# Attention whose products with v take float32 operands, in an order planned from a list of tasks

## The chip, the cores and the metric

The kernel runs on one core of a Trainium2 chip. The metric is the device time of one execution in microseconds (us). The engines are TensorE (PE, with its weight loads PEld), VectorE (DVE), ScalarE (ACT), GpSimd (POOL) and SyncE (SP), which issues the transfers (DMA). Each engine works through its own queue of instructions in the order in which the program was written.

## What is computed

Three blocks follow one another: attention over 4 batches of 12 heads (448 positions, 64 columns a head), a gated layer (768 to 1024, with a spatial product over the 448 positions), and a mixer (rank 32 over the positions, then 768 to 3072 and back).

```python
q_n, k_n = rmsnorm(q, g_q), rmsnorm(k, g_k)
scores = scale * (q_n @ k_n.T)
attn = exp(scores - max(scores))
x = (attn / (sum(attn) + 1e-9)) @ v        # 4 x 448 x 768
u, w = split(gelu(x @ w_in))               # 2 x 512
x = x + (u * (w_sg @ layernorm(w) * ... + b_sg)) @ w_out
t = x + (x.T @ U @ V).T
out = t + relu(t @ w_ch1) @ w_ch2
```

The large weights `w_in`, `w_out`, `w_ch1`, `w_ch2`, U and V arrive as float64 and are turned into float32 and then into two float16 halves on the chip (`from_f64`, `split_steps`). Nearly every large product is made of three products of float16 halves (high by high, high by low, low by high).

## The kernel before

**Units of attention.** A unit is a pair of heads of one batch: 24 units, 0 to 23. Its steps, in the names of the code: `load` and `load_v` (transfers for one to three units at a time), `sq` and `su` (squares on ACT, sums on DVE), `nw` (the reciprocal root, twelve steps on DVE, `rsqrt_steps`), `xn` (scaling, POOL), `ct` (eight float32 transposes of q and k on PE), `cq`, `ck`, `lq`, `lk` (their high halves on ACT, low halves on DVE), `cd` (eight transfers on SP that stack the halves into `kk` and `qq`), `mm` (eight matmuls that give an approximate maximum of each row of scores), `mr` (seven reductions on DVE), `mt`, `mn` (the maxima transposed, negated and sent into a row of `qq` by a transfer), `sc` (16 matmuls of the scores `st`), `se` (the exponential `e`, float32, on ACT), `sh` and `sl` (its halves `eh` on ACT and `el` on POOL), `va` and `vb` (the halves `vh` on ACT and `vl` on DVE of v, times 16, with a column of ones in `vh` for the sum), `pv` (96 matmuls into two banks, one a head: 8 groups of 128 output rows, each of 4 key blocks times 3 products) and `px` (the sum's reciprocal and the division into `XX`, DVE, for each head).

**Banks.** PE's results lie in 8 banks of 128 x 512 float32: the pool `ps` has 4 single banks (transposes, maxima and `pv` take turns), `pst` two tiles of two banks for the scores. When attention ends `pst` closes and a pool `ps2` of 2 banks takes its place.

**Order.** The table T of numbers gives each step of a unit a time, in units of `UT_` = 8.3 us; `at_unit` puts the step on a heap, and `issue()` takes the steps from the heap by time and writes their instructions. The first weights, the second half of `w_in` (`wv`: six tiles `wvh`, `wvl` of 128 x 512, which the first product behind attention needs), are spread over the times 21.12 to 23.715, that is, among the last units; their five conversion steps and both halves are on DVE (`alone`). The times of the work behind attention stand in the same table, and the stage of the mixer's last two products follows by rules of its own. Each tile converted by `from_f64` takes five operations: the absolute value or a mask, a clamp from below (L160), a shift, and two that join sign and low bits (L161 to L163).

Of the kernel before, what the change touches and what calls it, by code (L numbers as in the profile page):

```python
# [12 lines left out]
F16 = mybir.dt.float16  # L13
# [10 lines left out]
def attention_gmlp_mixer_kernel(  # L24
# [31 lines left out]
    P = 128  # L56
# [15 lines left out]
    ps = ctx.enter_context(tc.tile_pool(name="ps", bufs=4, space=PSUM))  # L72
# [9 lines left out]
    mhalf = const.tile([P, 14], F32, name="mhalf")  # L82
# [42 lines left out]

# [24 lines left out]
    def from_f64(m, z, alone):  # L150
        def f0():
            z["g"] = z["t"].bitcast(F32)
            if alone:
                nc.vector.tensor_scalar(out=z["t"], in0=z["d"][:, :, 1], scalar1=0x7FFFFFFF, scalar2=None, op0=ALU.bitwise_and)
            else:
                nc.scalar.activation(out=z["g"], in_=z["d"].bitcast(F32)[:, :, 1], func=AF.Abs)

        return [
            (dve2 if alone else act)(m, f0),
            dve2(m, lambda: nc.vector.tensor_scalar(out=z["g"], in0=z["g"], scalar1=2.0 ** -15 * 1.125, scalar2=None, op0=ALU.max)),  # L160
            dve2(m, lambda: nc.vector.tensor_scalar(out=z["t"], in0=z["t"], scalar1=3, scalar2=0x3FFFFFFF, op0=ALU.logical_shift_left, op1=ALU.bitwise_and)),  # L161
            dve(m, lambda: nc.vector.scalar_tensor_tensor(out=z["t"], in0=z["d"][:, :, 1], scalar=-0x40000000, in1=z["t"], op0=ALU.bitwise_and, op1=ALU.bitwise_or)),  # L162
            dve(m, lambda: nc.vector.scalar_tensor_tensor(out=z["w"].bitcast(I32), in0=z["d"][:, :, 0], scalar=29, in1=z["t"], op0=ALU.logical_shift_right, op1=ALU.bitwise_or)),  # L163
        ]
# [6 lines left out]

    def rsqrt_steps(y, x, t):

        yi, xi = y.bitcast(I32), x.bitcast(I32)
        steps = [
            lambda: nc.vector.tensor_scalar(out=yi, in0=xi, scalar1=1, scalar2=None, op0=ALU.logical_shift_right),
            lambda: nc.vector.tensor_scalar(out=yi, in0=yi, scalar1=-1, scalar2=0x5F3759DF, op0=ALU.mult, op1=ALU.add),
        ]
        return steps + 3 * [
            lambda: nc.vector.tensor_tensor(out=t, in0=y, in1=y, op=ALU.mult),  # L180
            lambda: nc.vector.scalar_tensor_tensor(out=t, in0=t, scalar=-0.5, in1=x, op0=ALU.mult, op1=ALU.mult),
            lambda: nc.vector.scalar_tensor_tensor(out=y, in0=t, scalar=1.5, in1=y, op0=ALU.add, op1=ALU.mult),
        ]
# [54 lines left out]

    def issue():


        rings = {x: SimpleNamespace(n=2, taken=[], back=set(), held=[]) for x in "dwx"}
# [4 lines left out]

        free = dict(V=0.0, A=0.0, G=0.0, D=0.0)
        done = set()
        running, waiting = [], []  # L250
        delay = 0.0
        heapq.heapify(jobs)
        while jobs or running:
# [14 lines left out]
            more.now = i  # L268
# [96 lines left out]
    def fp32_tile(name):  # L365
        return at.tile([P, 2 * S], F32, tag="e", name=name, bufs=EB)
# [943 lines left out]
```

## Time and profile before

| what | before |
|---|---|
| median of 2 runs | 1219.51 us (1218.91 to 1220.11) |
| the profiled execution | 1219.57 us, its span 1217.8 us |
| mean granted clock of PE | 0.972 |
| PE busy | 1152.3 us (95%) |
| PE weight loads busy | 627.4 us |
| DVE busy | 1017.6 us (84%) |
| ACT busy | 484.3 us (40%) |
| POOL busy | 390.6 us (32%) |

A row of a timeline has the start, the length, the engine, the line of the code, the operation, the tile written and the tiles read, the shape and the count; `x4` means that four neighbours stand in one row, whose length is that of all four. A group of rows by line has the busy time, the mean of one instruction, and the idle time of the engine ahead of it with what ended that. A window gives the busy time of each engine in a stretch, PE's granted clock (1.00 is full speed), the busy share of the 16 DMA engines and GB/s.

### The profile page before, as it was taken

Reading aid. Unit: us, or ns where it says so; the run is one execution under the profiler, and the core shown is the slowest. Engines: PE = TensorE matmul, PEld = TensorE weight load, DVE = VectorE, ACT = ScalarE, POOL = GpSimd, SP = SyncE. Lnnn points to the kernel's source line nnn. Section 1 sums busy time; section 2 is a strip of 40 time slices with the busy share of each in tenths; the row PEclk is TensorE's granted clock in tenths of the full one; section 3 lists DMA queues with packets and bytes.
Section 4 is the critical chain, followed back from the end, with each engine's and each line's share of the span. In section 5 each row is a group of like instructions: output and inputs, shape, how many; then the busy total and the mean of one; then the engine's idle time right before and its main releaser. Section 6 shows DMA issues by size and latency. Waiting matters only on the chain.

```text
span 1217.8 us, 20703 instructions
## 1 busy us (share of the span) xinstructions
PE 1152.3 (95%) x7914; PEld 627.4 (52%) x7914; DVE 1017.6 (84%) x2004; ACT 484.3 (40%) x850; POOL 390.6 (32%) x348
## 2 busy tenths in 40 slices
PE   8899999998579999996999999999999999999998
PEld 3355565554334454443445555555555555555554
DVE  6698999989988745789896998989879898898955
ACT  2677777765435322334342332323223232232200
POOL 3477777765333413674051111101111011110100
PEclk9799999998799999999999999999999999999999
DMA  5455544523546400435154222212222122212113
GB/s 139 118 131 132 124 110 117 130 72 106 137 113 139 119 1 1 95 84 115 25 117 91 63 87 73 69 49 74 61 62 58 59 67 69 61 57 61 44 65 117
DMA packets 134835, 103.88 MB, mean 85 GB/s; under 512 B 77328, under 2 KB 114896, under 8 KB 134736
## 3 DMA queue, kind: packets, MB, share of 16 engines
q1 hardware_dynamic: 134736, 102.56, 32.8%
q8 instruction: 62, 1.02, 0.4%
q14 instruction: 37, 0.30, 0.1%
HBM read 65.33 MB, written 5.51 MB: 58 GB/s over the span
## 4 chain that ended last, share of the span: by engine, by line
PE 67%; DVE 22%; DMA 4%; issue 3%; POOL 2%; ACT 2%; SPq 0%; DVEq 0%; ACTq 0%; POOLq 0%
PE pd L1172 8%; PE pd L1174 8%; PE pd L1173 8%; PE q L1111 7%; PE q L1112 6%; PE q L1113 6%; PE st L499 5%; PE pv L535 3%; PE pm L465 2%; DVE wt L162 2%; DVE ww L163 2%; DVE u L77 2%; PE won L361 2%; DVE wt L160 2%; DVE wt L161 1%
## 5 line engine op out<-in xcount | busy, mean ns | idle before, releaser
L1172 PE MATMUL pd<-w,hh 128*128 128x384 f16 x672 | 219.4, 326 | 2.6 <-ACT hh L1138 1.5
L1174 PE MATMUL pd<-w,hl 128*128 128x384 f16 x672 | 219.3, 326 | 1.3 <-DVE hl L1141 1.3
L1173 PE MATMUL pd<-w,hh 128*128 128x384 f16 x672 | 219.3, 326 | 0.5 <-DVE w L77 0.5
L1178 DVE SCALAR_TENSOR_TENSOR xx<-pd,xx 128x384 f32<-128x384 f32 x336 | 184.0, 551 | 25.9 <-PE pd L1174 23.0
L516 POOL TENSOR_TENSOR el<-e,eh 128x896 f16<-128x896 f32 (+1 forms) x96 | 165.3, 1733 | 69.5 <-ACT eh L510 62.0
L1111 PE MATMUL q<-u,w1h 128*128 128x448 f16 x504 | 178.7, 354 | 2.4 <-DMA u<-u 2.4
L1112 PE MATMUL q<-u,w1h 128*128 128x448 f16 x504 | 178.6, 354 | 0.0
L1113 PE MATMUL q<-u,w1l 128*128 128x448 f16 x504 | 178.5, 354 | 0.0
L1074 POOL TENSOR_TENSOR wt<-ww 128x256 f32<-128x256 f32 x36 | 27.3, 759 | 441.1 <-DVE ww L163 441.1
L536 PE MATMUL pv<-vl,eh 128*128 128x64 f16 (+1 forms) x768 | 113.3, 197 | 13.0 <-DVE vl L77 13.0
L1125 DVE TENSOR_TENSOR u<-q,u 128x448 f32<-128x448 f32 x144 | 87.7, 620 | 40.1 <-PE q L1113 38.0
L535 PE MATMUL pv<-vh,eh 128*128 128x65 f16 (+1 forms) x768 | 113.9, 201 | 0.0
L1138 ACT ACTIVATE hh<-u 128x448 f16<-128x448 f32 (+2 forms) x144 | 58.0, 445 | 136.9 <-DVE u L1125 136.8
L537 PE MATMUL pv<-vh,el 128*128 128x65 f16 (+1 forms) x768 | 112.1, 196 | 0.0
L470 DVE TENSOR_REDUCE mx<-pm 128x1 f32<-128x448 f32 x168 | 98.7, 619 | 12.3 <-PE pm L465 10.4
L499 PE MATMUL st<-qq,kk 128*128 128x448 f16 (+1 forms) x384 | 95.0, 384 | 0.3 <-DMA qq<-nm 0.3
L535 PEld LDWEIGHTS <-eh 128*128 128x128 f16 (+1 forms) x768 | 72.7, 98 | 40.6 <-issue 21.9
L1172 PEld LDWEIGHTS <-hh 128*128 128x128 f16 x672 | 65.6, 98 | 46.8 <-ACT hh L1138 2.3
L1174 PEld LDWEIGHTS <-hl 128*128 128x128 f16 x672 | 65.6, 98 | 46.5 <-DVE hl L1141 2.5
L1173 PEld LDWEIGHTS <-hh 128*128 128x128 f16 x672 | 65.6, 98 | 45.5 <-issue 2.2
L504 ACT ACTIVATE e<-st 128x896 f32<-128x896 f32 x96 | 77.1, 817 | 15.2 <-PE st L499 15.2
L510 ACT ACTIVATE eh<-e 128x896 f16<-128x896 f32 (+1 forms) x96 | 82.1, 855 | 0.2
(157 smaller groups left out, 2278.1 us busy)
## 6 DMA issues: line engine op xcount, KB each, us to landing
wd<-in_moe_w_ch_dram SPq DMA_DIRECT2D x36, 512.0 KB
wd<-in_moe_w_ch_dram SPq DMA_DIRECT2D x48, 384.0 KB
wd<-in_moe_w_in_dram SPq DMA_DIRECT2D x12, 512.0 KB
kk<-wk SPq DMA_DIRECT2D x48, 112.0 KB
qq<-wq SPq DMA_DIRECT2D x48, 112.0 KB
out_dram<-xx SPq DMA_DIRECT2D x12, 384.0 KB
raw<-in_q_dram SPq DMA_DIRECT2D x7, 576.0 KB
raw<-in_k_dram SPq DMA_DIRECT2D x7, 576.0 KB
```

Of the source, the lines that this page charges most:

```text
L499: nc.tensor.matmul(oo, kk[:, z, hh, cs], qq[:, z, hh, :], start=(z == 0), stop=(z == 1))
L516: (nc.vector if 4 * n + g in T["sd"] else nc.gpsimd).tensor_tensor(out=el[:, 0:m], in0=e, in1=Z[n][f"eh{g}"][:, 0:m], op=ALU.subtract)
L535: nc.tensor.matmul(o[:, g, :], ph, vh[kp, i, :], start=(kc == 0), stop=False)
L536: nc.tensor.matmul(o[:, g, 0:D], ph, vl[kp, i, :], start=False, stop=False)
L537: nc.tensor.matmul(o[:, g, :], pl, vh[kp, i, :], start=False, stop=(kc == 3))
L1111: nc.tensor.matmul(z[bank_], wh[:, c, b], uh[:, c], start=(c == 0), stop=False)
L1112: nc.tensor.matmul(z[bank_], wh[:, c, b], ul[:, c], start=False, stop=False)
L1113: nc.tensor.matmul(z[bank_], wl[:, c, b], uh[:, c], start=False, stop=(c == KH - 1))
L1172: nc.tensor.matmul(o[:, 0:HN], hh[:, m, ts], wh[:, m, ns], start=(m == GC - 1), stop=False)
L1173: nc.tensor.matmul(o[:, 0:HN], hh[:, m, ts], wl[:, m, ns], start=False, stop=False)
L1174: nc.tensor.matmul(o[:, 0:HN], hl[:, m, ts], wh[:, m, ns], start=False, stop=(m == 0))
L1178: then(e, [dve(HN, lambda z=z, ns=ns: nc.vector.scalar_tensor_tensor(out=X[i][:, ns], in0=z["o"][:, 0:HN], scalar=2.0 ** -14, in1=X[i][:, ...
```

## The change

- `pv` reads `e` and v as float32. A unit has 32 products in place of 96: 24 of 128 output rows and 8 of 64 rows, all of 65 columns, into one bank of 7 x 65 for both heads. `sh`, `sl`, `va` and `vb` are gone. Tiles `VR` hold v with its column of ones and with zeros where the half-height block of the other head stands; `load_v` needs five transfers in place of three.
- `px` runs once a unit for both heads.
- `ct` makes seven full transposes into one two-bank tile of `pst`. `mm` writes two blocks (i, i + 4) into a two-bank tile, `mr` reduces two banks at once (three of these, and one single).
- `nw` is two operations on POOL, the second a `pow`.
- `from_f64` loses the clamp: the first step multiplies by 2^-112 instead of taking the absolute value, so tiny values go to zero by themselves.
- `ps` has 2 banks, `pst` three tiles of two. Behind attention `ps2` and a new `ps3` take 2 banks each, and `bank` and `product` rotate over them.
- The order of attention comes from a list: `task(name, rank, engines, f, deps, ...)` names the step, its rank, the time it is taken to need on its engine, what must be done before, and which buffers of a counted ring it takes and gives back. `attention_order()` goes through time and starts, on each free engine, the ready task of the lowest rank. The six tiles of `wv` are chains of such tasks, with ranks spread over 21.12 to 23.715; their first step and high half are on ACT (`wva=0`). Ready tasks of lower rank go first, and where an engine would stand idle, a task of any rank may start. The times behind attention are moved by `SHIFT`, the planned end of attention less the old one; the next weights `wu` and `ws` wait until the last tile of `wv` is under way.

```diff
@@ from_f64
-                nc.scalar.activation(out=z["g"], in_=z["d"].bitcast(F32)[:, :, 1], func=AF.Abs)
+                nc.scalar.activation(out=z["g"], in_=src, func=AF.Copy, scale=2.0 ** -112)
-            dve2(m, lambda: nc.vector.tensor_scalar(out=z["g"], in0=z["g"], scalar1=2.0 ** -15 * 1.125, scalar2=None, op0=ALU.max)),
@@ load_v
-        dma(out=vr[:, :, 0:3, :], in_=v[b, h0:h0 + LH, 0:S3, :].rearrange("h (p c) d -> p h c d", c=3))
+        for c in range(3):
+            dma(out=vr[:, :, c, 0:D], in_=v[b, h0:h0 + LH, 0:S3, :].rearrange("h (p c) d -> p h c d", c=3)[:, :, c, :])
@@ nw
+        nc.gpsimd.tensor_scalar(out=ms, in0=ms, scalar1=1.0 / D, scalar2=1e-6, op0=ALU.mult, op1=ALU.add)
+        nc.gpsimd.tensor_tensor(out=y.rearrange("p u s -> p (u s)"), in0=ms, in1=mhalf[:, 0:14 * m], op=ALU.pow)
@@ ct
+        pt = pst.tile([P, 2, 512], F32, tag="st", name="pqk").rearrange("p a s -> p (a s)")
+        for o, c in ((0, 0), (1, 1), (2, 2), (3, 6), (4, 3), (5, 4), (6, 5)):
+            nc.tensor.transpose(out=pt[:, o * P:(o + 1) * P], in_=x[:, c, :], identity=ident)
@@ mm
+        pm = Z[n][f"pm{j}"] = pst.tile([P, 2, 512], F32, tag="st", name="pm")
+        for i in ((j, j + 4) if j < 3 else (3,)):
...
@@ pv
         for kc in range(4):
-            nc.tensor.matmul(o[:, g, :], ph, vh[kp, i, :], start=(kc == 0), stop=False)
-            nc.tensor.matmul(o[:, g, 0:D], ph, vl[kp, i, :], start=False, stop=False)
-            nc.tensor.matmul(o[:, g, :], pl, vh[kp, i, :], start=False, stop=(kc == 3))
+            for oo, e, cs in to:
+                i = 4 * e + kc if kc < 3 else 3
+                nc.tensor.matmul(oo, z[f"e{i // 2}"][:, i % 2, cs], v_[:, 4 * e + kc, :], start=(kc == 0), stop=(kc == 3))
@@ order
-    spread(UT_ * T["wv0"], UT_ * T["wv1"], wv[nw_:], T["wvl"], T["wvg"])
+        for g in range(4):
+            task(("sc", n, g), rk(f"s{g}", n), dict(P=(0.78, 0.97, 0.78, 0.4)[g]), lambda n=n, g=g: sc(n, g),
+                 [("md", n)] + [("cd", n, i) for i in range(4)], take=["st"])
...
+            task(("pv", n, hh, g), rk("ab"[hh] + str(g), n), dict(P=0.65 if g == 3 else 0.44), lambda n=n, hh=hh, g=g: pv(n, hh, g),
...
+    for c, steps in enumerate(wv):
+        chain(("wv", c), steps, T["wv0"] + (T["wv1"] - T["wv0"]) * c / KD, T["wvg"])
...
+    for t, x, e in (attn := attention_order())[0]:
+        at_time(t, x.f)
+    SHIFT = attn[1] - UT_ * T["te"]
```

PE's queue in the middle of attention, before: the products with v (`pv`) of one unit and a maximum's product (`pm`) of the next between two groups of them; a row is one instruction, and each matmul has its load of weights ahead of it.

```order
L537 LDWEIGHTS el
L537 MATMUL pv<-vh_110,el 128x65
L465 LDWEIGHTS wq
L465 MATMUL pm<-wk,wq 128x448
L535 LDWEIGHTS eh
L535 MATMUL pv<-vh_110,eh 128x65
L536 LDWEIGHTS eh
L536 MATMUL pv<-vl,eh 128x64
L537 LDWEIGHTS el
L537 MATMUL pv<-vh_110,el 128x65
```

PE's queue in the middle of attention, of the change: `vr_183` and `vr_184` are the v of two units, `pqk` the transposes of a later unit, `pmt` the transposed maxima.

```order
L523 MATMUL pv<-vr_183,e 128x65 x4
L503 LDWEIGHTS kk_98
L503 MATMUL st<-qq_101,kk_98 128x448
L503 LDWEIGHTS kk_98
L503 MATMUL st<-qq_101,kk_98 128x448
L523 MATMUL pv<-vr_183,e 64x65 x8
L424 MATMUL pqk<-ident,xn 128x128 x7
L476 MATMUL pmt<-ident,mx 7x128
L523 MATMUL pv<-vr_184,e 128x65 x4
L466 LDWEIGHTS wq
L466 MATMUL pm<-wk,wq 128x448
```

Twelve float16 products became four float32 ones (one row `x4`), the seven transposes stand in one row, and products of two units stand around each other.

DVE's queue among units 22 and 23, before: the five conversions and two halves of the first weights (L154 to L163, L114, L77) between the reductions `mx` of unit 23.

```order
L154 TENSOR_SCALAR wt<-wd 128x512
L470 TENSOR_REDUCE mx<-pm 128x1
L160 TENSOR_SCALAR wt<-wt 128x512
L161 TENSOR_SCALAR wt<-wt 128x512
L470 TENSOR_REDUCE mx<-pm 128x1
L162 SCALAR_TENSOR_TENSOR wt<-wd,wt 128x512
L470 TENSOR_REDUCE mx<-pm 128x1
L163 SCALAR_TENSOR_TENSOR ww<-wd,wt 128x512
L470 TENSOR_REDUCE mx<-pm 128x1
L114 TENSOR_SCALAR wvh<-ww 128x512
L77 SCALAR_TENSOR_TENSOR wvl<-ww,wvh 128x512
```

DVE's queue of the change, among the first units (the reduction `ms` is that of a later load):

```order
L400 TENSOR_REDUCE ms<-sq 128x14
L442 TENSOR_TENSOR wk<-pqk,wk 128x448
L161 TENSOR_SCALAR wt<-wt 128x512 x2
L162 SCALAR_TENSOR_TENSOR wt<-wd,wt 128x512 x2
L472 TENSOR_REDUCE mx<-pm 128x2 x2
L472 TENSOR_REDUCE mx<-pm 128x1
L472 TENSOR_REDUCE mx<-pm 128x2
L163 SCALAR_TENSOR_TENSOR ww<-wd,wt 128x512 x2
L77 SCALAR_TENSOR_TENSOR wvl<-ww,wvh 128x512
```

The same weights are now converted there, two tiles side by side and with four operations each on DVE, and none of `wvh`, `wvl` is left among the last two units.

## Rows read from the trace of the kernel before

**Rows 1.** Page: granted PE clock, tenths, 40 slices of 30.4 us.
```profile
PEclk9799999998799999999999999999999999999999
```

**Rows 2.** Windows, us: length; busy PE, PEld, DVE, ACT, POOL; clock; DMA
```profile
0.00:57.00 57.00, 48.78 (x265) 21.67 (x265) 37.07 (x83) 23.93 (x36) 23.06 (x24) 0.82 0.53 134
57.00:284.00 227.00, 217.95 (x2585) 130.79 (x2585) 207.25 (x450) 170.25 (x260) 168.41 (x100) 0.99 0.47 116
284.00:334.00 50.00, 31.77 (x336) 18.07 (x335) 48.54 (x83) 20.98 (x31) 18.70 (x10) 0.73 0.47 118
334.00:380.00 46.00, 39.04 (x188) 18.14 (x189) 39.88 (x84) 21.68 (x38) 16.75 (x21) 0.93 0.49 115
...
560.00:580.00 20.00, 11.13 (x62) 5.84 (x61) 19.90 (x31) 6.50 (x11) 10.38 (x9) 0.82 0.38 82
...
700.00:1180.00 480.00, 478.49 (x2745) 267.77 (x2744) 412.95 (x860) 136.63 (x289) 47.83 (x81) 1.00 0.20 61
```

**Rows 3.** PE timeline (start, length, us): first scores, units 2, 22, 23.
```profile
57.04 0.93 PE L499 MATMUL st<-qq,kk 128*128 128x448 f16 x4
...
283.40 0.93 PE L499 MATMUL st<-qq,kk 128*128 128x448 f16 x4
...
302.23 0.55 PE L499 MATMUL st<-qq,kk 128*128 128x448 f16 x2
```

**Rows 4.** DVE timeline: one first weight, and attention's last write.
```profile
317.64 0.69 DVE L77 SCALAR_TENSOR_TENSOR wvl<-ww,wvh 128x512 f16<-128x512 f32 x1
...
336.26 0.29 DVE L553 TENSOR_SCALAR xx<-pv,rd 64x64 f32<-64x64 f32 x1
```

**Rows 5.** PE timeline: maximum's products, scores, products with v.
```profile
21.99 0.56 PE L465 MATMUL pm<-wk,wq 64*128 64x448 f16 x4
...
101.97 0.93 PE L499 MATMUL st<-qq,kk 128*128 128x448 f16 x4
...
108.47 0.19 PE L535 MATMUL pv<-vh,eh 128*128 128x65 f16 x1
...
109.04 0.20 PE L535 MATMUL pv<-vh,eh 128*128 128x65 f16 x1
```

**Rows 6.** PE and its weight loads: float32 transposes, one more each.
```profile
100.61 0.44 PE L426 MATMUL pq<-ident,xn 128*128 128x128 f32 x2
...
100.61 0.55 PE L426 MATMUL pq<-ident,xn 128*128 128x128 f32 x3
...
100.61 0.14 PEld L426 LDWEIGHTS pq<-ident,xn 128*128 128x128 f32 x1
...
100.61 0.20 PEld L426 LDWEIGHTS pq<-ident,xn 128*128 128x128 f32 x2
```

**Rows 7.** DVE by line, 57 to 284 us: busy us, mean ns.
```profile
L470 DVE TENSOR_REDUCE mx<-pm 128x1 f32<-128x448 f32 x140 | 82.2, 619 | 9.5 <-PE pm L465 7.6
L77 DVE SCALAR_TENSOR_TENSOR vl<-vr,vh 128x448 f16<-128x448 f32 x20 | 32.5, 1623 | 0.1
L398 DVE TENSOR_REDUCE ms<-sq 128x14 f32<-128x896 f32 x17 | 18.0, 1056 | 0.0
L551 DVE TENSOR_TENSOR xx<-pv,rd 128x192 f32<-128x192 f32 x39 | 13.7, 351 | 0.7
...
L180 DVE TENSOR_TENSOR t<-y 128x42 f32<-128x42 f32 x18 | 11.2, 624 | 0.0
```

**Rows 8.** POOL by line, whole span: one column's addition and power.
```profile
L829 POOL TENSOR_TENSOR vr<-ve,mhalf 128x1 f32<-128x1 f32 x14 | 8.1, 579 | 1.2
L825 POOL TENSOR_SCALAR ve<-mv 128x1 f32<-128x1 f32 x14 | 5.0, 359 | 73.0 <-DVE mv L821 73.0
```

**Rows 9.** SP timeline: issue of one transfer.
```profile
106.25 0.60 SPq L453 DMA_DIRECT2D kk<-wk  x1
```

**Rows 10.** By line, whole span; then PE's waits, 380 to 700 us.
```profile
L160 DVE TENSOR_SCALAR wt<-wt 128x384 f32<-128x384 f32 (+2 forms) x106 | 48.7, 460 | 7.9 <-ACT wt L156 7.7
...
PE pa L940 <- DVE as L77: 8.9, 1, 8.9
```

More of the change, by code (lines that the diff above doesn't have):

```diff
@@ L246, in full @@
             return len(r.taken) >= r.n and r.taken[-r.n] not in r.back
+        ring_now.rings, ring_now.running, ring_now.now = rings, running, 0.0
         free = dict(V=0.0, A=0.0, G=0.0, D=0.0)
         done = set()
-        running, waiting = [], []
+        waiting = []
         delay = 0.0
@@ L590, in attention_gmlp_mixer_kernel @@
     for n in range(NU):
+        f0 = first[n]
         if n in size:
[L592 to L598 removed]
@@ L611, in attention_gmlp_mixer_kernel @@
-    wv = [weight(w_in, c * P, P, DH, DH, lambda c=c: (wvh[:, c, :], wvl[:, c, :]), 32.0, True) for c in range(KD)]
-    nw_ = int(T["wvn"])
-    spread(T["wa0"], T["wa0"] + T["wa1"] * nw_, wv[:nw_], T["wal"], T["wag"])
-    spread(UT_ * T["wv0"], UT_ * T["wv1"], wv[nw_:], T["wvl"], T["wvg"])
-    for i in range(7):
-        for j, f in enumerate(to_T(lambda: TA, i, 64.0)):
-            at_unit(T["tu"] + T["td"] * i + T["tt"] * j, f)
-    N = SimpleNamespace(ps2=None)
+            m = size[n]
+            prev = [k for k, _ in loads if 0 < k < n]
@@ new lines, in attention_gmlp_mixer_kernel @@
+            task(("ld", n), T.get(f"ld{n}", n + T["ld"]), dict(S=2.6), lambda n=n: load(n), take=["ms"] if n == 0 else ["ms", "raw"], lat=1.4 + 1.3 * m)
+            task(("lv", n), T.get(f"lv{n}", n + T["lv"]), dict(S=3.2), lambda n=n: load_v(n), take=[] if n == 0 else ["vr"], lat=1.6 + 0.7 * m)
+            task(("nw", n), rk("nw", n), dict(G=0.75 + 0.1 * m), lambda n=n: nw(n), [("su", n + i) for i in range(m)], take=["y"], give=[("ms", ("ld", n))])
+        last = n + 1 in size or n + 1 == NU
@@ new lines, in attention_gmlp_mixer_kernel @@
+        for hh, g in [(0, 0), (0, 1), (0, 2), (1, 0), (1, 1), (1, 2), (1, 3)]:
+            before = ("lv", f0) if hh == g == 0 else ("pv", n, 0, 0)
+            task(("pv", n, hh, g), rk("ab"[hh] + str(g), n), dict(P=0.65 if g == 3 else 0.44), lambda n=n, hh=hh, g=g: pv(n, hh, g),
+                 [before] + [("se", n, i) for i in ((0, 1), (1, 2, 3))[hh]], take=["o"] if hh == g == 0 else [])
+        pvs = [("pv", n, hh, g) for hh in range(2) for g in range(3)] + [("pv", n, 1, 3)]
+        task(("pvx", n), n - 9.0, dict(), None, pvs, give=([("vr", ("lv", f0))] if last and f0 else []) + [("e", ("se", n, g)) for g in range(4)])
@@ new lines, in attention_gmlp_mixer_kernel @@
+    wv = [weight(w_in, c * P, P, DH, DH, lambda c=c: (wvh[:, c, :], wvl[:, c, :]), 32.0, bool(T["wva"])) for c in range(KD)]
+    for c, steps in enumerate(wv):
+        chain(("wv", c), steps, T["wv0"] + (T["wv1"] - T["wv0"]) * c / KD, T["wvg"])
+    for i in range(7):
+        a_, v_, move = to_T(lambda: TA, i, 64.0)
+        bs = (0, 1) if i == 3 else (i // 4,)
+        rank = T["tu"] + T["td"] * i
+        task(("ta", i), rank, dict(A=0.75), a_[2], [("px", b * NHP + h, 3) for b in bs for h in range(NHP)], take=["s"])
+        task(("tv", i), rank + 0.1, dict(V=0.85), v_[2], [("ta", i)], lock=True)
+        task(("td", i), rank + 0.2, dict(S=1.3), move, [("tv", i)], lat=2.5, give=[("s", ("ta", i))])
```

385 lines of the change are left out of this document (240 added, 145 removed).

## The prediction

> **What bounds the kernel now.** I read the stages first. The slices of the whole span show where TensorE's (PE's) granted clock fell: in the first third, and nowhere behind it [rows 1]. Cut at the places where the work changes [rows 2], the first 334 us are attention, and from 700 to 1180 us PE is busy 478.49 of 480: nothing that this change touches can make that stretch shorter. What can be won lies in attention and the 300 us behind it. Attention has three parts. From unit 2's first score product at 57.04 us to unit 22's at 283.40 [rows 3], 20 units take 11.32 us each. PE is busy 217.95 us there, 10.90 a unit, and VectorE (DVE) 207.25, 10.36 a unit [rows 2]: both stand near the pace, PE nearer. Before it lies a start of 57 us at a mean clock of 0.82. Behind it, from 284 to 334 us, PE is busy only 31.77 of 50 us at clock 0.73 while DVE is busy 48.54: units 22 and 23 are 18.8 us apart [rows 3], since DVE turns the first weights (`wvh`, `wvl`) into halves between them, and ScalarE and PE wait for what stands behind these on DVE. The last result of attention is written at 336.55 [rows 4].
>
> **The products with v.** Now 12 float16 matmuls (3 products for each of 4 key blocks) take 0.57 us from one group to the next (108.47 to 109.04) [rows 5], 8 groups a unit, 4.56 us. After: 32 float32 matmuls of 65 columns. The trace has no plain float32 product, but float32 transposes of 128 columns: the third adds 0.11 us to the second, so a column costs 0.86 ns, and the next load of weights (0.14 us long) starts with the running matmul and hides under it [rows 6]. A transpose only passes values on, a product has to carry the low part too; I charge twice the column rate, 65 x 0.86 x 2 = 0.11 us, with the loads hidden: 32 x 0.11 = 3.52, a gain of **1.04 us a unit**. The bounds: below, one float16 pass, 0.57 / 12 = 0.05 us each; above, the eight transposes of a unit with their bare loads and turns, 1.36 / 8 = 0.17 (100.61 to 101.97), taken twice for a product, 0.34. I stay near the steady transposes, the only float32 rows. The Trainium skill ("FP8 and Floating Point Precision", TensorE Precision Notes) gives a true float32 product four passes; an estimate from that page, 4 x 65 columns at 2.4 GHz, is 0.108 us and would give 3.47 us a unit.
>
> One rule speaks against the change. The float32 load of weights lasts 0.14 us in the trace against the 0.10 of the float16 loads, but the second one starts 0.06 us after the first [rows 6], so by the rows a load every 0.055 us is possible and just covers a pass of 65 columns. The skill ("TensorE: Matmul & The Clock Gate", Weight-path perf modes) says that fast weight load is on for 128 weights only when they are not FP32. If loads came out from under the matmuls by that rule, the gain would turn; that is the first rival.
>
> **The other products.** Two rows of four transposes take 101.97 - 100.61 = 1.36 us a unit [rows 5, 6], since the half-height one breaks the row; seven full ones in a row cost 7 x 0.11 + 0.05 = 0.82: **0.54 less**. The maximum's products are issued in pairs of different heads. Where such pairs stood next to each other at the start, four took 0.56 us with their tail of some 0.16, two at a time [rows 5]; alone one takes 0.19 (448 columns). So up to 8 x 0.19 - 4 x 0.20 = 0.7 us, and nothing if banks or order keep them apart; I take **0.4**. PE per unit: 10.90 - 1.04 - 0.54 - 0.4 = **8.9 us**.
>
> **DVE and the other queues.** Removed from DVE: `vl` 32.5 / 20 = 1.62 us a unit, the Newton steps (the square alone 11.2 / 20 = 0.56), half of the small operations at the end of a unit (13.7 / 20 = 0.69 for the largest; I take 0.5). The maximum reads two banks at once: 896 columns took 1.06 us [rows 7], so 3 x 1.06 + 0.62 against 82.2 / 20 = 4.11: 0.3 less. 10.36 - 1.62 - 0.56 - 0.5 - 0.3 = 7.4. Added: the six first weights with four operations each, 0.69 us at most where nothing else holds them [rows 4], and seven splits of 768 columns, an estimate of 1.0 each from the 0.69 of 512; 24 us over 24 units, 1.0. So DVE stands at **8.4**, below PE. ScalarE and POOL lose the two splits of the probabilities and were not the bound. The reciprocal root goes to POOL, where the trace has only a `pow` of one column, 579 ns, beside an addition of one column of 359 [rows 8]: between 0.22 us (the difference) spread over the call and 0.58 for each of 42 columns; since the fixed part is plain in the addition, I take 4 us a load of three units at most, hidden under 29 us of PE. On SP each transfer takes 0.60 us to issue [rows 9]; a unit has 9 and a third of its loads, 9 of which v now has 5: 12 x 0.60 = 7.2 us a unit, also under PE. The smaller pieces of v move on 16 engines busy 47% in this stretch [rows 2]; taken as double the time of a v load they stay below that stretch's free half.
>
> **The sum.** Now pace / PE = 11.32 / 10.90 = 1.04. With PE at 8.9, DVE at 8.4 and SP at 7.2, all in one fixed order that the code plans from its own durations, I allow 10%: **9.8 us a unit** (bounds: 9.0, PE all but full; 10.8). The start: the 72 warming products and the first chain stay, so unit 0's scores again come near 29.5; two units at 9 us bring unit 2 to 47.5 instead of 57.04. Unit 23: 47.5 + 21 x 9.8 = 253.3. Its own rest is PE's 8.9 us for a unit, now unshared, and 2 for the last divisions (an estimate), 11 us: attention ends at **264.5 instead of 336.55, 72 us earlier**. The first weights are no longer between the last units, which is where 284 to 334 goes.
>
> Behind attention the order stays. Each weight tile loses one DVE operation: 106 x 0.46 = 48.7 us of DVE work [rows 10], nearly all under a busy PE from 600 us on, where it is worth nothing. It is worth something where PE waits: 8.9 us for `as` on a DVE that is busy 19.90 of 20 us at 560 to 580 [rows 2, 10], with some five of these ahead of it, and 7 us idle in 334 to 380. I take **6 us** (0 to 14). The wait for `as` itself is still there afterwards, shorter.
>
> 1217.8 - 72 - 6 = 1139.8 in the profiled execution's span; the run took 1219.57, 1.8 more, and the median 1219.51 is the same within 0.1: **1141 us**.
>
> **The rivals.**
> *The loads bind.* If a float32 load does not hide, a pass costs 0.055 + 0.055 and a product 0.22: 8.9 + 32 x 0.11 = 12.4 on PE, pace 12.9, attention ends at 54 + 21 x 12.9 + 13 = 338, only the 6 us behind it remain: 1219.5 + 1.5 - 6 = **1215**, no change. At the bare price, 0.34, PE needs 8.9 + 32 x 0.23 = 16.3, pace 16.9, the end is 60 + 21 x 16.9 + 15 = 430: 93 later, 6 of them given back behind it, **1307**, slower. From about 0.26 us a product on it is slower than now by more than 2%. For it: transposes are no products, and 65 columns cover half of what 128 do. Against: the loads 0.06 apart. Chances 0.07 and 0.04.
> *SP becomes the bound.* Its old 11 and a third transfers made 6.8 of 11.32 us; the rest it stood before transfers whose inputs were late. If half of these 4.5 us stay, the pace is 9.5, as forecast; if nearly all stay, 7.2 + 3.6 = 10.8, the end is 286, **1163**. Behind a waiting transfer stand the copies of the next unit's halves, and PE waits for these. Chance 0.10.
> *The root on POOL is slow.* At 0.58 us a column the first loads (14 and 28 columns) come 8 and 16 us late, later ones (24 us for three units) hide: **1157**. Chance 0.04.
>
> **How the numbers follow.** The forecast has 0.75, at 1141, own range 1116 to 1160 (a pace of 9.0 with 14 us behind attention, to one of 10.4 with none). With SP and POOL 0.89, so the range **1116 to 1182** leaves out the loads (0.11) and the tails of the rest; its upper end is the SP case with nothing won behind attention and 13 us more at the start. A measurement of this kernel tells some 2%, 24 us, from no change: faster by more 0.88, within it 0.08 (loads at 0.22 and what falls short), slower 0.04.
>
> **What would show it.** Products with v 0.11 us apart in a row; PE near 8.9 us a unit at a pace below 10.4; the last write of attention near 264; unit 23 no further behind unit 22 than the others; DVE not full there; `as` waited for, less than 8.9 us; from 700 us before the end the trace as before. A product at 0.2 or more, PE waiting for `qq` or `kk`, or a `pow` above 4 us would each show its rival. Wrong altogether it would be if attention ended early and PE then stood idle for weights: the gain would be given back behind it.

## The result, and the profile after

The changed kernel takes **1206.28 us** (1205.02 to 1207.55); its ratio to the kernel before is 0.9892, with an interval of 0.9842 to 0.9941. In a second set of runs it took 1207.96 us, ratio 0.9901 (0.988 to 0.9921). The forecast was 1141 us with a range of 1116 to 1182: the change is faster, by 13 us instead of 78. That is 1%, and the prediction gave a change of less than 2% a chance of 0.08.

The profiled execution has a span of 1203.2 us, 14.6 less than before. Two lines of its page, the busy time of the engines and the granted clock in 40 slices (compare [rows 1]):

```profile
PE 1155.2 (96%) x7122; PEld 674.0 (56%) x7122; DVE 881.8 (73%) x1610; ACT 411.8 (34%) x742; POOL 285.0 (24%) x277
...
PEclk9899999999999999998999999999999999999999
```

The windows after: length; busy PE, PEld, DVE, ACT, POOL; granted clock, DMA share, GB/s.

```profile
0.00:57.00 57.00, 48.82 (x280) 27.40 (x281) 26.92 (x38) 19.17 (x29) 32.32 (x33) 0.91 0.62 141
57.00:284.00 227.00, 213.48 (x1781) 158.19 (x1781) 156.37 (x255) 108.18 (x169) 74.50 (x30) 0.98 0.58 132
560.00:580.00 20.00, 19.03 (x86) 8.91 (x86) 15.04 (x29) 7.97 (x17) 3.14 (x5) 0.83 0.09 22
700.00:1180.00 480.00, 479.62 (x2760) 269.90 (x2760) 387.99 (x783) 133.55 (x281) 43.09 (x78) 1.00 0.21 63
```

From 57 to 284 us DVE went from 207.25 to 156.37 us and POOL from 168.41 to 74.50, as meant, but PE only from 217.95 to 213.48, and its weight loads rose from 130.79 to 158.19 [rows 2]. From 700 to 1180 us the trace is as before: PE is busy 479.62 of 480 us instead of 478.49.

PE's timeline after: the first scores of units 2, 22 and 23.

```profile
55.31 0.92 PE L503 MATMUL st<-qq,kk 128*128 128x448 f16 x4
...
294.47 0.92 PE L503 MATMUL st<-qq,kk 128*128 128x448 f16 x4
...
305.53 1.13 PE L503 MATMUL st<-qq,kk 128*128 128x448 f16 x4
```

DVE's timeline after: the last write of attention.

```profile
326.49 0.58 DVE L543 TENSOR_SCALAR xx<-pv,rd 64x64 f32<-64x64 f32 x2
```

The pace from unit 2 to unit 23 is (305.53 - 55.31) / 21 = 11.92 us a unit; the forecast was 9.8, and before it was (302.23 - 57.04) / 21 = 11.68 [rows 3]. Unit 23 now stands 11.1 us behind unit 22 and not 18.8. Attention ends at 327.07 instead of 336.55 [rows 4]; from there to the end of the span it is 876.2 us instead of 881.2.

Against the forecast end of attention, 264.5, the 62.6 us that are missing are: the start 55.3 - 47.5 = 7.8; the pace 21 x (11.915 - 9.8) = 44.4; and the tail behind unit 23's first score, 327.07 - 305.53 = 21.5 in place of 11, another 10.5. (The three make 62.7: the prediction's own terms, 253.3 and 11, add up to 264.3 and not 264.5.)

### The profile page after: what moved, and what is told of

It is laid out like the page before. It is cut to its first block, busy times and chain, and to the rows that moved or that the text cites. A ratio compares the mean times of both kernels' runs of the same rounds, so it can differ in the third digit from the quotient of the medians.

```text
span 1203.2 us, 18484 instructions
## 1 busy us (share of the span) xinstructions
PE 1155.2 (96%) x7122; PEld 674.0 (56%) x7122; DVE 881.8 (73%) x1610; ACT 411.8 (34%) x742; POOL 285.0 (24%) x277
## 4 chain that ended last, share of the span: by engine, by line
PE 82%; DVE 7%; DMA 4%; ACT 3%; POOL 2%; issue 2%; SPq 0%; ACTq 0%; DVEq 0%; POOLq 0%
PE pv L523 10%; PE pd L1312 8%; PE pd L1314 8%; PE pd L1313 8%; PE q L1251 7%; PE q L1252 7%; PE q L1253 7%; PE st L503 5%; PE pu L988 2%; PE won L356 2%; PE pu L990 2%; PE pu L989 2%; PE pm L466 1%; DMA qq<-nm 1%; PE pqk L424 1%
## 5 line engine op out<-in xcount | busy, mean ns | idle before, releaser
L523 PEld LDWEIGHTS pv<-vr,e 128*128 128x128 f32 (+1 forms) x1536 | 151.3, 179 | 21.0 <-issue 14.6
L523 PE MATMUL pv<-vr,e 128*128 128x65 f32 (+1 forms) x1536 | 159.6, 264 | 2.1 <-ACT e L508 1.3
L472 DVE TENSOR_REDUCE mx<-pm 128x2 f32<-128x896 f32 (+1 forms) x96 | 89.1, 970 | 29.4 <-PE pm L466 28.9
L503 PE MATMUL st<-qq,kk 128*128 128x448 f16 (+1 forms) x384 | 83.6, 372 | 9.4 <-DMA qq<-nm 4.8
L1251 PEld LDWEIGHTS <-w1h 128*128 128x128 f16 x504 | 49.7, 99 | 50.6 <-DMA u<-u 3.3
L1253 PEld LDWEIGHTS <-w1l 128*128 128x128 f16 x504 | 49.7, 99 | 46.9 <-issue 1.6
L1252 PEld LDWEIGHTS <-w1h 128*128 128x128 f16 x504 | 49.7, 99 | 45.9 <-issue 1.6
L1281 DVE SCALAR_TENSOR_TENSOR hl<-u,hh 128x448 f16<-128x448 f32 (+2 forms) x144 | 64.3, 471 | 12.1 <-ACT hh L1278 11.7
```

The costliest lines, as they stand in the source:

```text
L472: nc.vector.reduce_max(out=Z[n]["mx"][:, j:j + 4 * m - 3:4], in_=Z[n].pop(f"pm{j}")[:, 0:m, 0:S], axis=AX.X)
L503: nc.tensor.matmul(oo, kk[:, z, hh, cs], qq[:, z, hh, :], start=(z == 0), stop=(z == 1))
L523: nc.tensor.matmul(oo, z[f"e{i // 2}"][:, i % 2, cs], v_[:, 4 * e + kc, :], start=(kc == 0), stop=(kc == 3))
L1251: nc.tensor.matmul(z[bank_], wh[:, c, b], uh[:, c], start=(c == 0), stop=False)
L1252: nc.tensor.matmul(z[bank_], wh[:, c, b], ul[:, c], start=False, stop=False)
L1253: nc.tensor.matmul(z[bank_], wl[:, c, b], uh[:, c], start=False, stop=(c == KH - 1))
```

## The experiments

All times are medians beside runs of the kernel before on the same chip; the ratio and its 95% interval stand behind. "Pace" is that of units 2 to 23 in the profiled execution. The diffs are shortened, and `...` marks what is left out.

### What a float32 product costs

PE's timeline after, eight, nine and twenty passes of one row of products with v (each product is two passes, each with its own load of weights), and the twenty loads of weights (PEld):

```profile
209.10 1.11 PE L523 MATMUL pv<-vr,e 128*128 128x65 f32 x8 [0.67 <-ACT e L508]
...
209.10 1.22 PE L523 MATMUL pv<-vr,e 128*128 128x65 f32 x9 [0.67 <-ACT e L508]
...
209.10 2.45 PE L523 MATMUL pv<-vr,e 128*128 128x65 f32 x20 [0.67 <-ACT e L508]
...
209.10 2.31 PEld L523 LDWEIGHTS pv<-vr,e 128*128 128x128 f32 x20 [0.81 <-ACT e L508]
```

A pass takes (2.45 - 1.11) / 12 = 0.112 us and a product 0.223, not 0.11. A unit has 24 products of 128 rows and 8 of 64 that run two at a time: 24 x 0.223 + 0.6 = 6.0 us (the sixteen passes of the eight last 0.69 in a row with their tail), where the forecast had 3.52 and the kernel before 4.56.

**Half of the products.**

```diff
-        for kc in range(4):
+        for kc in (0, 3):
```

> Leaves out key blocks 1 and 2 of the products with v (half of the float32 products), so PE has half of that work; everything else stands as in the changed kernel, the order too. Theory 1 (the price of a float32 product is what failed: in the trace of the changed kernel a pair of passes takes 0.22 us, not 0.11, a unit 6.0 us, not 3.5): PE's 11.4 us a unit fall by 3.0 to 8.4, about what was forecast, the pace falls from 11.9 to about 9.2, attention ends near 268 in place of 327, time about 1146 us (1135 to 1160). Theory 2 (the order that was planned from durations that are wrong holds the pace, or another engine does): less than 20 us is won, 1187 or more.

Measured: 1178.88 us, 0.9646 (0.9628 to 0.9663), pace 11.04. That is between the two theories: 27 us of the 60 came. The price of the products counts, but something else holds the pace at 11. Part of it is the clock: from 57 to 284 us it is 0.89 in place of 0.98, and PE is still busy 191.36 us, 9.3 a unit and not 8.4.

**Fewer columns.** The products move 33 columns; the division on DVE writes each result twice.

```diff
-nc.tensor.matmul(oo, z[...][:, i % 2, cs], v_[:, 4 * e + kc, :], ...)
+nc.tensor.matmul(oo[:, 32:65], z[...][:, i % 2, cs], v_[:, 4 * e + kc, 32:65], ...)
```

> The products with v read and write only columns 32 to 64 of v (33 in place of 65, the ones among them; the output's first 32 columns repeat the others). Theory 1a (each of the two passes shows a load of 0.055 us that does not hide, and then 0.86 ns a column): a pass takes 0.055 + 0.028 = 0.083, a product of 128 rows 0.17 in place of 0.22, a unit 1.5 us less, time about 1172 (1165 to 1182). Theory 1b (the loads hide and a column costs 1.7 ns): a pass takes 0.056, a product 0.11, a unit 2.9 less, time about 1145 (1135 to 1155).

Measured: 1255.82 us in the three executions on which the ratio rests, 1.0297 (1.023 to 1.0365). Neither theory holds. PE's timeline of this kernel, four and five passes of 33 columns:

```profile
72.67 0.63 PE L523 MATMUL pv<-vr,e 128*128 128x33 f32 x4
...
72.67 0.74 PE L523 MATMUL pv<-vr,e 128*128 128x33 f32 x5
```

A pass still takes 0.74 - 0.63 = 0.11 us at full clock. Half the columns save nothing, so neither columns nor a sum of load and columns is the price. What is left is **the load of 128 columns of float32 weights, with 65 columns hidden beneath it**, or a fixed time of a pass; the next experiment tells these apart. The kernel became slower although a pass costs the same, and its clock had fallen, as a window of it shows (same columns as above):

```profile
160.00:180.00 20.00, 20.00 (x87) 13.24 (x89) 9.56 (x14) 4.48 (x7) 4.09 (x3) 0.53 0.25 52
```

PE is busy 20.00 of 20 us and the granted clock is 0.53, nearly all at the lower level of 1.2 GHz. Why it fell under a busy PE is not shown.

**Two products of 64 rows for one of 128.** The arithmetic is the same.

```diff
-            to = [(o[:, 3 * hh + g, :], hh, slice(g * P, (g + 1) * P))]
+            to = [(o[a * 64:a * 64 + 64, 3 * hh + g, :], hh, slice(g * P + a * 64, g * P + a * 64 + 64)) for a in range(2)]
```

> Each float32 product of 128 output rows is made as two of 64 rows that stand next to each other (the same arithmetic, twice the instructions). In the changed kernel's trace the products of the last 64 rows of both heads run two at a time, and their pairs of passes are 0.058 us apart with the loads hidden. Theory 1a (the load of 128 columns is what shows, and of two 64-row products the load of one runs beside the other): 24 x 2 x 0.06 + 0.5 = 3.4 us a unit in place of 6.0, pace about 9.5, time about 1148 (1138 to 1165). Rival (the two halves take turns): 24 x 4 x 0.058 + 0.5 = 6.1, time 1206 as before, or slower by the doubled instructions.

Measured: 1187.76 us, 0.973 (0.9708 to 0.9752), pace 10.96, and attention ends at 306.8. PE's timeline of this kernel, 36 and 54 passes of 64 rows:

```profile
138.41 1.27 PE L523 MATMUL pv<-vr,e 128*64 128x65 f32 x36
...
138.41 1.79 PE L523 MATMUL pv<-vr,e 128*64 128x65 f32 x54
```

18 passes take 0.52 us, 0.029 each; the four that replace one product take 0.116 us, half the price, about the 0.11 that was forecast. In the trace two passes, one for each half of the array, start within 0.01 us of each other, and the next two 0.058 later. So a load of 64 columns takes half the time of one of 128, and the loads for the two halves run side by side; a fixed time of 0.11 us a pass would have given 0.22. Theory 1a has the price right, 3.4 us a unit, and the time wrong, 1188 for 1138 to 1165. From 57 to 284 us (windows, columns as above) PE now needs

```profile
57.00:284.00 227.00, 194.20 (x2897) 122.53 (x2893) 162.69 (x271) 115.66 (x179) 74.56 (x30) 0.96 0.61 139
```

194.20 us for 227 / 10.96 = 20.7 units, 9.4 a unit, in part at a lower clock. PE has come near the 8.9 of the forecast, and the pace has not come near 9.8.

### What holds the pace then

PE's waits in the kernel with 64-row products, 57 to 284 us (total, times, longest):

```profile
PE st L503 <- DMA qq<-nm: 21.1, 8, 6.1
PE st L503 <- DVE mx L472: 2.9, 4, 1.3
```

`qq<-nm` is the transfer of the negated maxima, 1.8 KB. The longest wait, on PE's timeline:

```profile
118.63 0.35 PE L503 MATMUL st<-qq,kk 128*128 128x448 f16 x1
125.11 1.28 PE L503 MATMUL st<-qq,kk 128*128 128x448 f16 x3 [6.13 <-DMA qq<-nm]
```

ScalarE's timeline: the maxima were ready at 115.0.

```profile
114.77 0.25 ACT L480 ACTIVATE nm<-pmt 7x128 f16<-7x128 f32 x1
```

SP's queue between (start, length of the issue):

```profile
114.60 2.25 SPq L190 DMA_TRANSPOSE t<-s  x1
116.95 0.57 SPq L370 DMA_DIRECT2D raw<-in_q_dram  x1
117.57 1.08 SPq L371 DMA_DIRECT2D raw<-in_q_dram  x1
118.71 0.60 SPq L370 DMA_DIRECT2D raw<-in_k_dram  x1
119.36 0.64 SPq L371 DMA_DIRECT2D raw<-in_k_dram  x1
120.09 0.82 SPq L483 DMA_DIRECT2D qq<-nm  x1
```

The transfer of the maxima is issued 5.1 us late, behind a transposing transfer of 2.25 us and four loads of q and k, and lands another 4 us later. The list scheduler had planned 1.3 us for the transposing transfer and 1.6 for the landing.

**The maxima on ScalarE's queue.**

```diff
-        dma(out=QQ[n % 2][D:D + 1, 1]...)
+        nc.scalar.dma_start(out=QQ[n % 2][D:D + 1, 1]...)
-        task(("md", n), rk("mn", n), dict(S=0.65), ...)
+        task(("md", n), rk("mn", n), dict(A=0.1), ...)
```

> The products made as two of 64 rows, and in addition the transfer of the negated maxima into qq (1.8 KB a unit) is issued on ScalarE's queue, right behind the operation that makes it, instead of on SP. With the 64-row products the trace shows PE waiting 21.1 us in 8 places for this transfer, up to 6.1 us; in the longest it stood 5.1 us on SP behind a transposing transfer and four loads of q and k (1.3 MB), and landed 4 us after its issue. Theory 1 (SP's queue is what holds the pace once the products are cheap): these waits go but for the transfer's own 2 us, attention ends some 15 us earlier, 1173 us (1165 to 1180). Theory 2 (the data lies in the same 16 DMA engines behind the loads, or the next step of the chain is as late): less than 6 us is won, 1182 or more.

Measured: 1179.55 us, 0.968 (0.9653 to 0.9707). The waits for `qq<-nm` fall from 21.1 to 10.2 us, the pace only to 10.93; the start is 3.7 us earlier. Neither theory holds: 1179.55 lies in the range of theory 1, but attention ends 2.7 us earlier (304.1 for 306.8) and not 15, and the start alone would explain that.

**The root for each unit by itself**, on top of it (`nw` on 14 columns, its task once a unit). The list's duration for four products also goes from 0.44 to 0.5 in this run.

> As the run before, and the reciprocal root is taken for each unit by itself (14 columns, 2.6 us in the trace) instead of for a load of three (42 columns, 7.1 us). Theory 1 (the root of the third load stands in the start's chain, 41.2 to 48.2 us): unit 3's transposes come some 4.5 us earlier, and the end some 3 to 5 us earlier than in the run before. Theory 2 (PE has other work at that time): within 2 us of the run before.

Measured: 1187.84 us, 0.9747 (0.9721 to 0.9774). Unit 2 starts 1.1 us earlier, but the order that follows has a pace of 11.42. Both theories miss. Any edit moves the whole list, and here the order lost more than the edit won; which of the two edits moved it is not shown.

**No loads of v** from unit 9 on; then **v's loads issued by POOL** (their task in the list is on POOL too, 5.0 us in place of 3.2 on SP); then POOL and the maxima on ScalarE together.

```diff
+        if n >= 9:
+            ...
+            return
```

```diff
-            dma(out=vr[:, :, c, 0:D], ...)
+            nc.gpsimd.dma_start(out=vr[:, :, c, 0:D], ...)
```

> The products made as two of 64 rows, and the loads of v left out from the load of unit 9 on (the products read the v that is there), so SP has five transfers fewer a load and the DMA engines 0.7 MB less, in the small pieces that the change brought. All else is as in the run with 64-row products (1188 us, PE waits 21 us for qq<-nm). Theory 1 (SP and the DMA engines behind it hold the pace once the products are cheap): these waits fall to less than 10 us and the time to 1178 or less. Theory 2 (the chain from the maxima to the scores is late by its own steps on DVE, PE and ACT): within 4 us of 1188.

Measured: 1184.46 us, 0.9711 (0.9679 to 0.9743); PE still waits 22.2 us for `qq<-nm`. Theory 2: the small pieces of v are not the cause.

> The products made as two of 64 rows, the loads of v issued by POOL instead of SP; the same bytes move. Theory 1a (SP's queue, the order in it): as without these loads, 1178 or less. Theory 1b (the 16 DMA engines, where a small transfer stands behind large ones): 1188 within 4, although the loads of v have gone in the run before. POOL is busy a third of the time, so its 5 us of issue for three units are covered.

Measured: 1199.45 us, 0.9839 (0.9817 to 0.9862).

> Both at once: the negated maxima sent from ScalarE's queue (1180 us alone) and the loads of v issued by POOL. Theory 1a: some 5 us less than either, 1172 to 1178. Theory 1b: 1180 within 3.

Measured: 1191.64 us, 0.9773 (0.975 to 0.9796). Both miss their theories and are slower than without POOL: unit 2 starts at 59.6 and 58.4 instead of 55.5 and 51.8. On POOL's timeline the issues of v's transfers stand ahead of the first root, which starts at 18.23 in place of 10.29. Behind the start the pace is 11.32 and 11.15, no better: taking v off SP's queue this way does not help.

**A quarter of the products**, 64 rows each: the test whether PE's work sets the pace at all.

```diff
-        for kc in range(4):
+        for kc in (3,):
...
-                nc.tensor.matmul(..., start=(kc == 0), stop=(kc == 3))
+                nc.tensor.matmul(..., start=True, stop=(kc == 3))
```

> 64-row products, and only the fourth key block of each (a quarter of the products; the rest is left out): PE has some 6.5 us of work a unit in place of 9.0. Order and all else as in the run with 64-row products (1188 us, pace 10.97). Theory 1 (the chain maxima, transposition, transfer, scores and SP's queue hold the pace): pace 10.5 to 11, 1175 to 1190, more waits for qq. Theory 2 (PE's work still sets it, with a share of waits on top): pace 8.5, 1137 or less.

Measured: 1173.17 us, 0.9612 (0.9592 to 0.9632), pace 10.71. The window from 57 to 284 us and the waits of PE in it:

```profile
57.00:284.00 227.00, 166.41 (x1265) 80.34 (x1263) 162.58 (x271) 119.15 (x184) 74.44 (x30) 0.89 0.62 142
```

```profile
PE st L503 <- DMA qq<-nm: 28.4, 13, 6.4
PE st L503 <- DVE mx L472: 10.4, 11, 2.2
```

PE is busy 166.41 us in place of 194.20, and the pace falls by 0.25 us. Theory 2 is refuted: with cheap products the amount of PE's work does not set the pace. That the chain from the maxima over the transfer to the scores does, as theory 1 has it, is not shown by this run: PE waits there, but a wait that is taken away can come back elsewhere, as it does below when the waits for `qq<-nm` fall by two thirds. The clock was 0.89, so that PE needed 7.9 us a unit and not 6.5.

### The order

**The scheduler's durations corrected** in the changed kernel (four products 0.9 us, the root 0.25 + 2.35 a unit).

```diff
-dict(P=0.65 if g == 3 else 0.44)
+dict(P=0.65 if g == 3 else 0.9)
-dict(G=0.75 + 0.1 * m)
+dict(G=0.25 + 2.35 * m)
```

> The list scheduler is given measured durations: 0.9 us for four float32 products in place of 0.44, 0.25 + 2.35 us per unit for the root on POOL in place of 0.75 + 0.1. Nothing else changes, only the order that follows. Theory 1 (PE is full, 95% of 60 to 320 us): at most its idle 11 us can be won, 1195 to 1210. Theory 2 (the wrong durations cost the time): 20 to 60 us are won, 1146 to 1186.

Measured: 1245.05 us, 1.0199 (1.0172 to 1.0226), slower, which neither theory had: pace 13.30. PE's timeline of this kernel around one wait:

```profile
182.07 1.11 PE L523 MATMUL pv<-vr,e 128*128 128x65 f32 x8
...
190.10 0.35 PE L503 MATMUL st<-qq,kk 128*128 128x448 f16 x1
192.50 0.73 PE L503 MATMUL st<-qq,kk 128*128 128x448 f16 x3 [2.04 <-DMA qq<-nm]
...
199.76 1.97 PE L523 MATMUL pv<-vr,e 128*128 128x65 f32 x8
```

After 2.04 us without work the same eight passes take 1.97 us instead of 1.11. The window behind it:

```profile
200.00:210.00 10.00, 10.00 (x47) 8.05 (x49) 1.60 (x2) 1.46 (x3) 0.00 (x0) 0.50 0.00 0
```

The granted clock is 0.50, the lower level, while PE is busy all the time. So here PE paid for the wait and then for the clock behind it. Truer durations for PE and POOL did not make the better order; the transfers' stayed as they were.

**Float16 products in the new order** (the split of `e` and v as before, as tasks; room for 3 tiles `e` in place of 8, and 6 of each half; the list's durations for the products changed with them).

> The changed kernel with the products with v on float16 halves again (12 products of 0.0475 us for four key blocks; eh on ScalarE, el on POOL, vh on ScalarE, vl on VectorE, as tasks of the list), in the new order with all else of the change. Theory 1 (float32 loads are what failed): a unit's products need 4.0 us in place of 6.0, PE 9.4 a unit, and the time comes to 1180 to 1195, as with 64-row products, whose pace of 11.0 other things set. Theory 2 (the new order itself is worth little, and the work that went with the float32 products from ScalarE, POOL and VectorE was the gain): POOL has 10 us a unit and becomes the bound, 1205 or more.

Measured: 1247.45 us, 1.0227 (1.021 to 1.0244), pace 13.98. PE's waits, 57 to 284 us:

```profile
PE st L503 <- DMA qq<-nm: 27.7, 11, 5.5
PE pv L547 <- POOL el L520: 12.5, 4, 6.4
```

Theory 2 in its direction, but it cannot be put down to one cause: the splits on POOL stand beside the root there, and there are fewer buffers.

**The transfers' durations corrected, the first weights late**, both on 64-row products: each alone, the first together with the maxima on ScalarE's queue, and both together.

```diff
-        task(("td", i), rank + 0.2, dict(S=1.3), ...)
+        task(("td", i), rank + 0.2, dict(S=2.6), ...)
-        task(("md", n), ..., lat=1.6, ...)
+        task(("md", n), ..., lat=2.6, ...)
```

```diff
-        chain(("wv", c), steps, ..., T["wvg"])
+        chain(("wv", c), steps, ..., T["wvg"], [("px", 18, 3)])
```

> 64-row products; the scheduler is told 2.6 us in place of 1.3 for a transposing transfer on SP, and 2.6 in place of 1.6 us until the maxima's transfer lands. Only the order changes. Theory 1 (SP's planned order holds the pace): the waits for qq<-nm fall below 12 us of 21, 1172 to 1182. Theory 2 (orders differ by chance, none reaches the forecast pace): 1180 to 1200 with another set of waits.

Measured: 1179.82 us, 0.9672 (0.9648 to 0.9696). The time stands where the two ranges meet, and the rest speaks for theory 2: the waits for `qq<-nm` are 18.1 us and not below 12, and the pace is 11.07. The gain is in the start, unit 2 at 50.3 in place of 55.5.

> 64-row products; the first weights only behind unit 18's divisions. With the products as in the change this won 6 us (1200). Theory 1 (their 512 KB loads and the work on VectorE and ScalarE stood ahead of the maxima's chain): again 5 to 8 us, 1180 to 1183. Theory 2: with cheap products the last units lack the room, 1188 or more.

Measured: 1179.55 us, 0.9682 (0.9662 to 0.9702), pace 10.63, with waits for `qq<-nm` of 19.9 us: theory 1 in the time, and the gain is in the pace.

> 64-row products, the maxima sent from ScalarE's queue, and the scheduler told 2.6 us for the transposing transfer and for the maxima's landing. Theory 1: the waits for qq fall below 8 us in all, 1168 to 1176, the best of all here. Theory 2: within 4 us of 1180.

Measured: 1181.51 us, 0.9695 (0.9645 to 0.9744): no better than either, pace 10.91. PE's waits, 55 to 290 us:

```profile
PE pm L466 <- ACT wk L434: 7.0, 3, 3.6
PE st L503 <- DMA qq<-nm: 6.8, 4, 2.9
PE st L503 <- DMA qq<-wq: 3.8, 3, 1.7
```

The sign of theory 1 is there, waits for `qq<-nm` of 6.8 us (with the 64-row products alone they were 21.1 in the same stretch), and the gain is not: the pace was 10.96 and is 10.91. Other waits stand in their place, for the halves of k and for the transfers of those of q. So the late transfer of the maxima is where PE waited, and not by itself what holds the pace.

> 64-row products, the first weights behind unit 18, and the scheduler told 2.6 us for the transposing transfers on SP and for the landing of the maxima. Each alone gave 1180. If they take away different waits: 1170 to 1175. If what is left is the chain itself: within 4 us of 1180.

Measured: **1169.05 us**, 0.9568 (0.9545 to 0.9591), attention ends at 296.8. The two edits add up, since they act in different places: the start is that of the first (unit 2 at 50.4), the pace that of the second (10.64). This is the fastest kernel here that leaves nothing out. Its waits for `qq<-nm` are 9.8 us, where the late first weights alone had 19.9 at the same pace; its window:

```profile
57.00:284.00 227.00, 199.77 (x3056) 129.87 (x3054) 166.81 (x280) 117.72 (x183) 73.97 (x30) 0.95 0.61 138
```

### The other terms

**The clamp back** (`from_f64` as before).

> The changed kernel with the conversion from float64 as it was before (five operations, the clamp among them). Theory 1 (the clamp's DVE time is worth the 5 us by which the stage behind attention became shorter): attention as in the changed kernel plus about nothing (DVE is 75% busy there), from its end to the kernel's end 5 us more, 1211 us (1207 to 1216). Theory 2 (the 5 us come from the banks or from the order behind attention): 1206 within 2 us.

Measured: 1202.33 us, 0.9876 (0.9831 to 0.9921): not theory 1, and 4 us below theory 2's 1206. From the end of attention to the end of the span it is 875.9 us with the clamp and 876.2 without. PE's longest wait behind attention, after and with the clamp back:

```profile
PE pa L1079 <- DVE as L77: 7.7, 1, 7.7
```

```profile
PE pa L1078 <- DVE as L77: 8.8, 1, 8.8
```

One us is won at the wait, and nothing at the end.

**The first weights late**, in the changed kernel.

> The changed kernel, but the first weights (wv) may start only when unit 18's divisions are done, so that they stand among the last five units again, as before. Theory 1 (their early place is worth what lay between units 22 and 23): DVE needs 6 x 3 us for them in the last 60 us, which has room (DVE 21 of 40 us busy at 300 to 340), so only 0 to 6 us are lost, 1206 to 1214. Theory 2 (they hold up the last units as they did before): attention ends 15 to 20 us later, 1221 to 1228.

Measured: 1200.24 us, 0.9848 (0.9825 to 0.9871). Neither theory has it faster. Attention ends at 318.0 instead of 327.1, and 4 us of it are given back behind. The early place is worth nothing; it costs 6 to 8 us (1206.28 and 1207.96 less 1200.24).

**The changed kernel again**, for these two.

> The changed kernel once more, beside the three runs below on one chip and the kernel before: 1206 us within 4. The runs with the clamp back (1202) and with the late first weights (1200) are read against it.

Measured: 1207.96 us, 0.9901 (0.988 to 0.9921).

## Why the prediction was wrong, by its steps

**The products with v** are the step that failed. It read [rows 6] as "a column costs 0.86 ns, and the next load of weights (0.14 us long) starts with the running matmul and hides under it". In those rows a transpose loads 128 columns of float32 weights and moves 128 columns every 0.11 us, and the rows cannot tell which of the two sets that pace. The products of 33 columns and of 64 rows together can: it is the load. With 65 columns to move, the load is bare, and a product has two. The gain of 1.04 us a unit became a loss of 6.0 - 4.56 = 1.44: 2.5 us a unit, 52 us over 21 units.

This is the first rival, "the loads bind" at 0.22, which had a chance of 0.07 and 1215 us. It was dismissed with "the second one starts 0.06 us after the first", but two loads are not yet a rate. In the trace before, the third load ends 0.31 - 0.20 = 0.11 us behind the second [rows 6]:

```profile
100.61 0.31 PEld L426 LDWEIGHTS pq<-ident,xn 128*128 128x128 f32 x3
```

The rival's price was right by luck: it added 0.055 for a load to 0.055 for the columns, and the load alone takes 0.11. Its time was 9 us too slow. Its pace was 12.9 and not 11.92, mainly since the eight half-height products cost 0.6 in all and not 8 x 0.22; its rest behind unit 23's first score, 13 us instead of 21.5, gave part of that back. The Trainium skill ("TensorE: Matmul & The Clock Gate", Weight-path perf modes) excludes FP32 from the fast weight load, and the trace agrees: 0.11 us for a float32 load of 128 columns, against 0.0475 for a float16 product with its load [rows 5]. The four passes that the Trainium skill ("FP8 and Floating Point Precision", TensorE Precision Notes) gives a true float32 product made an estimate of 0.108 us. Here 0.223 was measured, and the measurement decides.

**The other products** came out nearly as forecast: PE has 213.48 us for 227 / 11.92 = 19.0 units, 11.2 us a unit, 5.2 without the products, where 10.90 - 4.56 = 6.3 stood before; 1.1 less, 0.94 forecast. **DVE** was right too: 156.37 / 19.0 = 8.2, forecast 8.4.

**The pace.** "I allow 10%" put 9.8 upon 8.9. The kernels with cheap products show 10.6 to 11.4 in seven orders (those with v's loads on POOL left aside), and 10.7 with a quarter of the products. So even with the right price the forecast would have failed: the kernel with that price takes 1188 us. This is the second step that failed. What holds the pace there stayed open. SP, the second rival, had nearly the right pace, 10.8, but its reason is not borne out. A transfer that PE needs did stand behind others on SP; yet with that transfer on ScalarE and the waits for it down from 21.1 to 6.8 us the pace was 10.91, without the loads of v on SP it was 11.03, and with 64-row products SP's issues add up to 173 of the 227 us from 57 to 284, not to all. Of the edits that leave nothing out, only the late first weights lowered the pace clearly: from 10.96 to 10.63, and in the changed kernel from 11.92 to 11.51.

**The start.** The root was to take "4 us a load of three units at most, hidden under 29 us of PE". POOL's timeline after, for 14, 28 and 42 columns:

```profile
10.35 2.62 POOL L407 TENSOR_TENSOR y<-ms,mhalf 128x14 f32<-128x14 f32 x1
...
15.91 4.81 POOL L407 TENSOR_TENSOR y<-ms,mhalf 128x28 f32<-128x28 f32 x1
...
41.15 7.08 POOL L407 TENSOR_TENSOR y<-ms,mhalf 128x42 f32<-128x42 f32 x1
```

A column costs 0.16 us, and 42 take 7.08. The third load's root stands in the start's chain (41.15 to 48.23), and unit 2 comes at 55.3 and not at 47.5; unit 0's first score is already 2.9 us later than forecast (32.4 for 29.5). The root's place in the order weighs more than its length. With the transfers' durations corrected, on 64-row products, the same 42 columns start 7 us earlier:

```profile
34.17 7.08 POOL L407 TENSOR_TENSOR y<-ms,mhalf 128x42 f32<-128x42 f32 x1
```

There unit 2 comes at 50.3, where 64-row products alone leave it at 55.5; the root for each unit by itself won 1.1 us. Later roots hide, as forecast.

**The tail.** The forecast had "PE's 8.9 us for a unit, now unshared, and 2". PE from unit 23's first score to the end, by line:

```profile
L523 PE MATMUL pv<-vr,e 128*128 128x65 f32 (+1 forms) x132 | 13.0, 261 | 0.0
L947 PE MATMUL pvv<-wvh,t 128*128 128x512 f16 x11 | 4.2, 381 | 0.3 <-DVE xx L543 0.3
```

These are the products with v of two units (132 passes; a unit has 64), and the first weights' products (8 us with their second line), which also stood there before. The forecast counted one unit and no first weights. The 21.5 us are PE's work and not a wait: it is busy 21.2 of them.

**Behind attention** 6 us were forecast and 5.0 came, but not from the clamp: with it back the stretch is as short. Where they come from stayed open. **The first weights** no longer part units 22 and 23, as forecast, but not because they are early: late, units 22 and 23 are 10.5 us apart.

## What to carry to other kernels

A row of a matmul that loads as many columns as it moves does not say which of the two is the price: look for a row where they differ before it is used for another shape. Float32 products with 65 or 33 moving columns paid here for two bare loads of weights, and two products of 64 output rows beside each other halved that. Where an engine is relieved, a share of overhead on top of its work is no forecast of the pace: a quarter of the products left it at 10.7 us. And the largest wait in a trace is not yet the bound: here the waits for a 1.8 KB transfer fell by two thirds and the pace stayed.

## What the runs showed of the hardware

The time of a float32 pass did not change between 65 and 33 moving columns (0.11 us each), and loads for the two halves of the array run side by side (0.116 us for four passes of 64 rows). With less to move, the granted clock fell to 0.53 under a PE busy 20.00 of 20 us, and the kernel with half the columns (1256 us) was some 4% slower than the one with all (1208). A wait of 2.04 us was followed by a stretch at 0.50. A `pow` on POOL took 0.16 us a column (14, 28 and 42 columns). What holds the pace near 10.6 to 11.4 us once the products are cheap, what the 5 us behind attention are due to, and why the truer plan for PE and POOL gave the worse order, stayed open.
